# Two batches, then one, then one: another order of the MLPs beside attention, and 24 heads without split probabilities

## The chip, the core and the metric

The kernel runs on one core of one Trainium2 chip. The metric is device time in microseconds (us), from three runs of the same program. The profile and the trace come from a fourth execution. The engines are named as in the profile: PE (TensorE; PEld is its weight load), DVE (VectorE), ACT (ScalarE), POOL (GpSimd), SP (the queue that issues every DMA here).

## What is computed

Attention over 4 batches of 12 heads, 448 rows of 64, with normalised queries and keys; its output, 1792 rows of 768, goes through two MLPs.

```python
q_n, k_n = rmsnorm(q, g_q), rmsnorm(k, g_k)
scores = q_n @ k_n.T / sqrt(64)
attn = exp(scores - max)
attn = attn / (attn.sum(-1) + 1e-9)
x = attn @ v                          # 4 x 448 rows, 12 heads x 64 = 768 columns
h = x @ w_in                          # 768 -> 2048
x = maximum(0.01 * h, h) @ w_out      # 2048 -> 768
a, b = x @ w1, x @ w2                 # 768 -> 1024, twice
out = (a * b @ w3) @ w_out2           # 1024 -> 1024 -> 768
```

The MLP weights come in as float64.

## The kernel before

**Split products.** PE multiplies in a reduced float32 (`F32R`). To keep float32 accuracy, an operand is split into a high part, its rounding, and a low part, the rest; a product is then three matmuls, high by high, low by high and high by low (`group`, lines 516 to 518). ACT makes the high part, DVE or POOL the low part by a subtraction (`subtract`, line 183; `split` for activations).

**Attention**, one head at a time (`attention_steps`). Step s issues the values of head s - 2, the transposes of the probabilities of head s - 1, and the scores of head s, each in four chunks of 112 rows, then loads and preparation of later heads. `scores` (lines 263 to 276): two matmuls into `ps`, DVE scales them to `p`, ACT takes the exponent. `p_transpose` (line 307): four PE transposes into `pt`, of which there are two buffers; then either ACT copies `pt` to `pth` and DVE subtracts to get `ptl`, or, for the first `WHOLE` heads, one copy, by DVE for two chunks and by ACT for two, keeps the probabilities in full float32. `values`: split heads take eight `F32R` matmuls of 128 columns of weights, `[vh | vl]`, into `po` (line 361), and the two halves are added; the first `WHOLE` heads take four float32 matmuls on unsplit values `v_whole` (line 349). For split heads the values `v` themselves are split by ACT and POOL (`vs`). Normalised outputs of batches 0 and 1 are split at once into the tiles `xh`, `xl` of that batch; those of batches 2 and 3 go to `xd` in DRAM and are read back when their MLP begins.

**Weights.** `Weights` hands out tiles of 128 by 768 or 128 by 512, in the order in which a list names them. A wide (float64) tile is turned into float32 in two halves: per half two operations on ACT (lines 457, 462), two on POOL (458, 463), one on DVE (459); the result is written to DRAM (`kept_...`) for the next pass. Every tile is then split into `wh` on ACT (line 479) and `wl`, on POOL for wide ones, else on POOL or DVE in turn. Two tiles are made ahead; there are three buffers each of `raw`, `wh` and `wl`.

**The MLPs.** First, `combine_weights` multiplies the last two weight matrices (`pw`, 384 matmuls of 384 columns). `first_mlp` has four groups; each takes four tiles of w_in to four hidden blocks (`t`, `y`, `gh`, `gl`), then six tiles of w_out, added to `acc`. `second_mlp` has two groups of eight tiles of w1 and w2 and six of the combined weights `wc`. A tile serves as many batches as go together: `product` multiplies it into one `ps_mm` (three buffers) for each. A batch needs 1008 MLP matmuls of 448 columns.

**What sets the order.** `fill` walks through the attention steps and issues a plan's MLP work between them, evenly over the plan's slots (a slot is one head's ten steps). A scheduler then orders each engine's instructions by a timeline that it makes at build time, by readiness and the priorities in `PRIORITY`; on the chip each engine runs its list in that order. Before, `COMBINE_SLOTS` puts the combining beside heads 5 to 16, `early` two groups of batch 0's first MLP up to slot 25, `late` the same groups of batch 1 and then everything else of batches 0 and 1 beside the other heads, and `rest`, batches 2 and 3 together, behind attention.

Of the kernel before, what the change touches and what calls it, by code (L numbers as in the profile page):

```python
# [17 lines left out]
B, H, S, D = 4, 12, 448, 64  # L18
# [6 lines left out]
NG = 4  # L25
# [3 lines left out]
PB = 2  # L29
KH2 = K2 // 2  # L30
NO = DM // P
NH = B * H
# [4 lines left out]
KEYS_AHEAD = 5  # L37
GROUPS = {0: 2, 2: 2, **{i: 4 for i in range(4, 48, 4)}}
MAX_GROUP = 4
WHOLE = 8  # L40
COMBINE_SLOTS = 5, 17
EARLY = 2
PRIORITY = dict(
    values=200, p_transpose=600, scores=600, prep=600, load=100, statistics=100, keys=50
)
# [3 lines left out]
def attention_then_moe(  # L49
# [41 lines left out]
    def copy(eng, out, x):  # L91
        if eng == "A":
            nc.scalar.activation(out, x, AF.Copy)  # L93
        elif eng == "V":
            nc.vector.tensor_copy(out, x)
        else:
            nc.gpsimd.tensor_scalar(out, x, 1.0, 1.0, op0=ALU.mult, op1=ALU.mult)
# [73 lines left out]
    def load_v(i):  # L171
        if i >= NH:
            return
        b, j = divmod(i, H)
        if i < WHOLE:
            heads[i]["v"] = att.tile([CP, NCH, D], F32, tag="vs", name="v_whole")
# [65 lines left out]
    def v_split(i):  # L242
        if not 0 <= i < NH or i < WHOLE:
            return
        h = heads[i]
        h["vs"] = att.tile([CP, NCH, 2, D], F32R, tag="vs", name="vs")
        copy("A", h["vs"][:, :, 0], h["v"])
        subtract("P", h["vs"][:, :, 1], h["v"], h["vs"][:, :, 0])
# [49 lines left out]
    def p_transpose(i, kc):  # L298
        if not 0 <= i < NH:
            return  # L300
        h = heads[i]
        tags = ("pth",) if i < WHOLE else ("pth", "ptl")
        dt = F32 if i < WHOLE else F32R
        h[f"pt{kc}"] = tuple(att.tile([CP, S], dt, tag=tag, name=tag, bufs=3) for tag in tags)
# [9 lines left out]
        def natural(x):  # L314
            return x.rearrange("k (p c) -> k p c", c=NCH)

        if i < WHOLE:
            copy("VVAA"[kc], natural(h[f"pt{kc}"][0]), pt)
# [15 lines left out]
    def values(i):  # L334
# [11 lines left out]
        x = h["x"]  # L346
        if i < WHOLE:
            for kc in range(NCH):
# [174 lines left out]
    def combine_weights(ws, hi, lo):  # L523
        def last(half):
            for _ in range(KH2):
                while ws.ready <= ws.taken:
                    with tc.high_priority(CONVERT_PRIORITY if ws.ready else 0):
                        next(ws.pieces)
                    yield CONVERT_NS
                ws.take()  # L530

        n = DM // 2
        for k in range(K2):
            ps = [ps_mm.tile([P, 512], F32, tag="mm", name="pw") for _ in range(2)]
            for half in range(2):
                if k == 0:
                    yield from last(half)
                w = ws.take()
                js = range(half * KH2, (half + 1) * KH2)
                for e in range(2):  # L540
                    cols = slice(e * n, (e + 1) * n)
                    xs = [(hi[:, j, cols], lo[:, j, cols]) for j in js]
                    yield from group(ws, ps[e], n, w, xs, first=half == 0, last=half == 1)
            for e in range(2):
                o = att.tile([P, S], F32, tag="t", name="wo", bufs=1)[:, :n]
                nc.scalar.activation(o, ps[e][:, :n], AF.Copy)  # L546
                nc.sync.dma_start(
                    wc[3 * e : 3 * e + 3, :, k].rearrange("m p c -> p m c"),
                    o.rearrange("p (m c) -> p m c", m=3),
                )  # L550
# [102 lines left out]
    def sources(plan):  # L653

        kept = {}
        for f, bs, g in plan:
            if f is first_mlp:
                tiles = [w_in[g * KG + m] for m in range(KG)] + [w_out[g, m] for m in range(NO)]
            else:
                tiles = [w12[g * KH2 + m // 2, m % 2] for m in range(2 * KH2)]  # L660
            if (f, g) in kept:
                yield from ((k, False, None, None) for k in kept[f, g])
            else:
                kept[f, g] = [
                    dram.tile([P, w.shape[1] // 2], F32, name=f"kept_{f.__name__}{g}_{i}")
                    for i, w in enumerate(tiles)
                ]
                yield from ((w, True, k, None) for w, k in zip(tiles, kept[f, g]))
            if f is second_mlp:
                for m in range(NO):  # L670
                    w = wc[m, :, g * KH2 : (g + 1) * KH2].rearrange("p k c -> p (k c)")
                    yield w, False, None, None

    def plan_ns(plan):
        n = {first_mlp: KG * KD + NO * KG, second_mlp: 2 * KH2 * KD + NO * KH2}
        return sum(3 * S * NS * len(bs) * n[f] for f, bs, _ in plan)
# [22 lines left out]
    per_slot = 2 * NCH + 2  # L699
    slots = COMBINE_SLOTS  # L700

    def fill(gen, total, span, until, begin=0):

        spent, n = 0.0, 0
        done = False
        while True:
            at = next(steps, None)
            n += 1
            while not done and spent < total * (n - begin) / span:
                c = next(gen, None)  # L710
                if c is None:
                    done = True
                else:
                    spent += c
            if at is None or at == until:
                break
        for _ in gen:
            pass

    parts_of = [(first_mlp, g) for g in range(NG)] + [(second_mlp, g) for g in range(2)]  # L720
    early = [(f, (0,), g) for f, g in parts_of[:EARLY]]
    late = [(f, (1,), g) for f, g in parts_of[:EARLY]]
    late += [(f, (0, 1), g) for f, g in parts_of[EARLY:]]
    rest = [(first_mlp, (2, 3), g) for g in range(NG)]
    rest += [(second_mlp, (2, 3), g) for g in range(2)]

    def run(pool, ws, plan):
        for f, bs, g in plan:
            yield from f(pool, ws, bs, g)

    with tc.tile_pool(name="comb", bufs=1) as pool:
        hi = pool.tile([P, K2, DM], F32R, name="lasth")
        lo = pool.tile([P, K2, DM], F32R, name="lastl")
        ws = Weights(
            [
                w
                for k in range(K2)
                for h in range(2)
                for w in [
                    (w_last[j], True, None, (hi[:, j], lo[:, j]))  # L740
                    for j in range(h * KH2, (h + 1) * KH2)
                    if k == 0
                ]
                + [(w3t[k, h], True, None, None)]
            ]
            + list(sources(early + late + rest))
        )
        n = slots[1] - slots[0]
        fill(combine_weights(ws, hi, lo), comb_ns, n * per_slot, slots[1], slots[0] * per_slot)
    pool = ctx.enter_context(tc.tile_pool(name="mlp", bufs=1))  # L750
    n = PB * H + 1
    fill(run(pool, ws, early), plan_ns(early), (n - slots[1]) * per_slot, n)
    fill(run(pool, ws, late), plan_ns(late), (B - PB) * H * per_slot, None)
    fill(run(pool, ws, rest), plan_ns(rest), 1, None)


# [42 lines left out]
```

## Time and profile before

| | |
|---|---|
| median of 3 runs | 1305.79 us (1301.84 to 1306.22) |
| the profiled execution | 1304.23 us |
| its span, first to last instruction | 1302.3 us |
| mean granted clock of PE | 0.963 |
| busy: PE, DVE, ACT, POOL | 1198.4, 691.5, 705.9, 710.4 us |

Busy time of PE counts each matmul from its start to its modelled end, and matmuls overlap. So the useful measure is how far apart matmuls start. The granted clock is 1.00 for 2.4 GHz and 0.50 for 1.2 GHz; between the two it is a mean over a stretch. The rows on which the prediction rests stand in a section of their own below.

### The profile page before, as it was taken

The numbers are of one execution on the slowest core, as the hardware profiler recorded it, in microseconds if no ns is written. First come the engines' busy times: TensorE is split into PE (matmuls) and PEld (weight loads), VectorE is DVE, ScalarE is ACT, GpSimd is POOL, SyncE is SP. The second block draws the span as 40 slices with busy tenths as digits, with TensorE's granted clock in tenths as the row PEclk, the third lists the DMA queues.
The fourth block names the chain that finished last, engine by engine and source line by source line (L and its number), as shares of the span: only waits on it lengthen the run. The fifth ranks groups of instructions, "written<-read, shape, count | busy, mean of one in ns | idle before, by whom it ended". The sixth has DMA issues, their size and how long they took to land.

```text
span 1302.3 us, 18390 instructions
## 1 busy us (share of the span) xinstructions
PE 1198.4 (92%) x5960; PEld 1046.6 (80%) x5960; DVE 691.5 (53%) x1323; ACT 705.9 (54%) x1551; POOL 710.4 (55%) x723
## 2 busy tenths in 40 slices
PE   3988988997789999979988999999999999999998
PEld 2436877776679778868877998999999999999998
DVE  6786676777878697755884445333123232211112
ACT  6776677788758576656755576433331323323220
POOL 6787666898844369866986357444131314421120
PEclk8789998998889999999988999999999999999999
DMA  8677656667665456654555244144212121211112
GB/s 240 174 176 205 174 168 191 189 203 210 186 188 161 125 166 182 205 165 135 159 150 184 75 129 139 59 145 131 65 41 66 41 65 45 73 45 60 59 37 93
DMA packets 108576, 172.67 MB, mean 133 GB/s; under 512 B 23776, under 2 KB 62656, under 8 KB 108480
## 3 DMA queue, kind: packets, MB, share of 16 engines
q1 hardware_dynamic: 108480, 171.50, 45.5%
q8 instruction: 47, 0.77, 0.2%
q14 instruction: 49, 0.40, 0.1%
HBM read 130.45 MB, written 30.45 MB: 124 GB/s over the span
## 4 chain that ended last, share of the span: by engine, by line
PE 52%; DMA 16%; DVE 11%; POOL 7%; issue 6%; ACT 4%; SPq 2%; POOLq 0%; DVEq 0%; ACTq 0%
PE ps_mm L516 15%; PE ps_mm L517 15%; PE ps_mm L518 15%; DVE raw L459 3%; DMA w<-w 3%; DMA ks<-kt_sb 2%; DMA w<-w_out 2%; POOL raw L463 2%; PE pt L307 2%; DVE p L267 2%; PE po L361 2%; DMA kt_sb<-kt 2%; DMA rk<-rs 2%; POOL wl L183 1%; DMA w<-w_in 1%
## 5 line engine op out<-in xcount | busy, mean ns | idle before, releaser
L516 PE MATMUL ps_mm<-xh,wh 128*128 128x448 f32 x768 | 284.7, 371 | 0.7 <-ACT wo L546 0.7
L517 PE MATMUL ps_mm<-xl,wh 128*128 128x448 f32 x768 | 284.5, 371 | 0.0
L518 PE MATMUL ps_mm<-xh,wl 128*128 128x448 f32 x768 | 283.5, 370 | 0.0
L183 POOL TENSOR_TENSOR wl<-raw,wh 128x512 fp32r<-128x512 f32 (+1 forms) x105 | 164.7, 1568 | 180.7 <-ACT wh L479 163.0
L183 POOL TENSOR_TENSOR gl<-y,gh 128x448 fp32r<-128x448 f32 x96 | 113.3, 1181 | 192.8 <-ACT gh L93 189.4
L516 PE MATMUL ps_mm<-gh,wh 128*128 128x448 f32 x576 | 210.7, 370 | 5.3 <-ACT wh L479 2.5
L479 ACT ACTIVATE wh<-raw 128x512 fp32r<-128x512 f32 (+1 forms) x172 | 122.9, 715 | 164.9 <-PE ps_mm L517 159.4
L518 PE MATMUL ps_mm<-gh,wl 128*128 128x448 f32 x576 | 211.0, 369 | 0.0
L517 PE MATMUL ps_mm<-gl,wh 128*128 128x448 f32 x576 | 210.6, 368 | 0.0
L463 POOL TENSOR_TENSOR raw<-raw,w 128x384 uint32<-128x384 uint32 (+1 forms) x160 | 157.2, 993 | 42.6 <-DVE raw L459 35.1
L307 PE MATMUL pt<-ident,p 112*112 112x112 f32 x768 | 117.9, 279 | 44.5 <-DVE ptl L183 27.2
L516 PEld LDWEIGHTS ps_mm<-xh,wh 128*128 128x128 f32 x768 | 146.4, 191 | 12.8 <-ACT wo L546 1.1
L459 DVE SCALAR_TENSOR_TENSOR raw<-raw,w 128x384 uint32<-128x384 uint32 (+1 forms) x160 | 127.6, 813 | 54.3 <-POOL w L458 50.3
L517 PEld LDWEIGHTS ps_mm<-xl,wh 128*128 128x128 f32 x768 | 146.8, 191 | 11.8
L518 PEld LDWEIGHTS ps_mm<-xh,wl 128*128 128x128 f32 x768 | 146.3, 191 | 12.0
L307 PEld LDWEIGHTS pt<-ident,p 112*112 112x112 f32 x768 | 90.0, 142 | 81.9 <-DVE ptl L183 32.5
L276 ACT ACTIVATE p<-p,low 112x448 f32<-112x448 f32 x192 | 126.9, 662 | 48.8 <-DVE p L267 48.7
L267 DVE TENSOR_SCALAR_CACHE_REDUCE p<-ps,rs 112x448 f32<-112x448 f32 x192 | 125.3, 676 | 39.3 <-PE ps L264 22.6
L183 DVE TENSOR_TENSOR wl<-raw,wh 128x512 fp32r<-128x512 f32 (+1 forms) x67 | 58.4, 872 | 141.0 <-ACT wh L479 139.7
L462 ACT ACTIVATE w<-w 128x384 uint32<-128x384 uint32 (+1 forms) x160 | 78.5, 492 | 94.2 <-DMA w<-w 32.9
L183 DVE TENSOR_TENSOR ptl<-pt,pth 112x448 fp32r<-112x448 f32 x160 | 96.9, 617 | 58.6 <-ACT pth L93 57.6
L516 PEld LDWEIGHTS ps_mm<-gh,wh 128*128 128x128 f32 x576 | 109.3, 190 | 17.7 <-ACT wh L479 3.2
(75 smaller groups left out, 1991.0 us busy)
## 6 DMA issues: line engine op xcount, KB each, us to landing
w<-w_in SPq DMA_DIRECT2D x32, 384.0 KB, 4.7
w<-w_out SPq DMA_DIRECT2D x48, 256.0 KB, 3.7
w<-w SPq DMA_DIRECT2D x32, 384.0 KB, 4.3
qk_sb<-qk SPq DMA_DIRECT2D x48, 224.0 KB, 3.9
qt_sb<-qt SPq DMA_DIRECT2D x96, 112.0 KB, 3.2
raw<-kept_first_mlp SPq DMA_DIRECT2D x24, 384.0 KB, 3.5
raw<-kept_first_mlp SPq DMA_DIRECT2D x36, 256.0 KB, 2.7
w<-w3t SPq DMA_DIRECT2D x32, 256.0 KB, 3.7
```

The source lines that it names most:

```text
L183: e.tensor_tensor(out, x, y.bitcast(F32), op=ALU.subtract)
L267: nc.vector.tensor_scalar(p, ps, h["scale"][:, c : c + 1], None, op0=ALU.mult, op1=ALU.min, accum_out=low,)
L276: exps[i] = nc.scalar.activation(p, p, AF.Exp, bias=low, scale=-1.0, accum_out=h["sum"][:, c : c + 1])
L307: nc.tensor.transpose(pt[:, c * CP : (c + 1) * CP], h["p"][c][:, kc * CP : (kc + 1) * CP], ident[:CP, :CP],)
L361: nc.tensor.matmul(po[:, :S], v, h[f"pt{kc}"][e], start=(kc == 0 and e == 0), stop=(kc == NCH - 1 and e == 1),)
L459: nc.vector.scalar_tensor_tensor(top, top, 3, high, op0=ALU.logical_shift_left, op1=ALU.bitwise_or)
L462: nc.scalar.activation(low, low, AF.Copy, scale=2.0**-29)
L463: nc.gpsimd.tensor_tensor(top, top, low, op=ALU.add)
L479: nc.scalar.activation(flat[0], x, AF.Copy)
L516: nc.tensor.matmul(ps[:, :n], wh[:, k], xh, start=(first and k == 0), stop=False)
L517: nc.tensor.matmul(ps[:, :n], wh[:, k], xl, start=False, stop=False)
L518: nc.tensor.matmul(ps[:, :n], wl[:, k], xh, start=False, stop=end)
```

## The change

`WHOLE` goes from 8 to 24, so heads 8 to 23 (the rest of batch 0, and batch 1) keep their probabilities and values unsplit. The combining is spread over slots 5 to 24 in place of 5 to 17. The plans `early`, `late` and `rest` go; three others come, each with both MLPs whole: batches 0 and 1 together over slots 25 to 37, batch 2 alone over slots 37 to the end of attention, batch 3 alone behind it. Each plan passes through all the weights: wide tiles in the first, kept float32 tiles in the two others. Batches 2 and 3 now alternate between the two sets of activation tiles.

```diff
-WHOLE = 8
-COMBINE_SLOTS = 5, 17
-EARLY = 2
+WHOLE = 24
+COMBINE_SLOTS = 5, 24
+MLP_SLOTS = 25, 37, NH + 2
...
-    parts_of = [(first_mlp, g) for g in range(NG)] + [(second_mlp, g) for g in range(2)]
-    early = [(f, (0,), g) for f, g in parts_of[:EARLY]]
-    late = [(f, (1,), g) for f, g in parts_of[:EARLY]]
-    late += [(f, (0, 1), g) for f, g in parts_of[EARLY:]]
-    rest = [(first_mlp, (2, 3), g) for g in range(NG)]
-    rest += [(second_mlp, (2, 3), g) for g in range(2)]
+    def whole(*bs):
+        return [(first_mlp, bs, g) for g in range(NG)] + [(second_mlp, bs, g) for g in range(2)]
+
+    plans = whole(0, 1), whole(2), whole(3)
...
-            + list(sources(early + late + rest))
+            + list(sources([part for plan in plans for part in plan]))
...
-    n = PB * H + 1
-    fill(run(pool, ws, early), plan_ns(early), (n - slots[1]) * per_slot, n)
-    fill(run(pool, ws, late), plan_ns(late), (B - PB) * H * per_slot, None)
-    fill(run(pool, ws, rest), plan_ns(rest), 1, None)
+    fill(iter(()), 0, 1, MLP_SLOTS[0])
+    for plan, begin, end in zip(plans, MLP_SLOTS, MLP_SLOTS[1:] + (None,)):
+        span = (end - begin) * per_slot if end else 1
+        fill(run(pool, ws, plan), plan_ns(plan), span, end)
```

In the built order, these are PE's instructions at the scores of head 21, before. `xh` and `wh` are the high parts of activations and weights in the first MLP.

```order
L307 MATMUL pt<-ident,p 112x112 x5
L361 MATMUL po<-ptl,vs 128x448
L307 MATMUL pt<-ident,p 112x112 x4
L516 MATMUL ps_mm<-xh,wh 128x448
L517 MATMUL ps_mm<-xl,wh 128x448
L307 MATMUL pt<-ident,p 112x112 x4
L361 MATMUL po<-pth,vs 128x448
L361 MATMUL po<-ptl,vs 128x448
```

The same place of the changed kernel's PE order:

```order
L263 MATMUL ps<-ks,qh 112x448
L264 MATMUL ps<-ks,ql 112x448
L307 MATMUL pt<-ident,p 112x112 x8
L263 MATMUL ps<-ks,qh 112x448
L264 MATMUL ps<-ks,ql 112x448
L349 MATMUL po<-pth,v_whole 64x448 x2
L307 MATMUL pt<-ident,p 112x112 x3
L349 MATMUL po<-pth,v_whole 64x448
```

MLP matmuls no longer stand between the transposes, and the values are float32 matmuls. On PE, 72 MLP matmuls stand ahead of the last scores of head 26, in place of 338, and 2607 ahead of those of head 47, in place of 1694; the combining ends among the scores of head 18, in place of head 16.

On DVE near head 20, before (`raw` is a weight tile that is being turned into float32, `rs` and `rt` belong to the statistics of later heads):

```order
L459 SCALAR_TENSOR_TENSOR raw<-raw,w_3592 128x384
L183 TENSOR_TENSOR ptl<-pt,pth 112x448
L267 TENSOR_SCALAR p,low<-ps,rs 112x448
L107 TENSOR_SCALAR rs<-ss 112x32
L267 TENSOR_SCALAR p,low<-ps,rs 112x448
L459 SCALAR_TENSOR_TENSOR raw<-raw,w_3594 128x384
L110 TENSOR_SCALAR rs<-rs 112x32
L459 SCALAR_TENSOR_TENSOR raw<-raw,w_3660 128x384
L183 TENSOR_TENSOR ptl<-pt,pth 112x448
```

and of the changed kernel:

```order
L144 TENSOR_SCALAR rs<-rs 112x16
L267 TENSOR_SCALAR p,low<-ps,rs 112x448
L95 COPY pth<-pt 112x448 x2
L267 TENSOR_SCALAR p,low<-ps,rs 112x448
L230 SCALAR_TENSOR_TENSOR kt_sb<-kt_sb,gqk,rk_sb 128x448
```

The weights' halves are gone from DVE here, and a copy stands where a subtraction that waits for ACT's copy stood.

Last, PE behind attention in the changed kernel, where batch 3's hidden blocks of a group end (the numbers are buffers: `gh_12866` is the last hidden block, `wh_12821`, `wh_12848` and `wh_12879` are three weight tiles):

```order
L517 MATMUL ps_mm_12891<-gl_12809,wh_12848 128x448
L518 MATMUL ps_mm_12891<-gh_12808,wl_12849 128x448
L516 MATMUL ps_mm_12912<-gh_12692,wh_12879 128x448
L517 MATMUL ps_mm_12912<-gl_12693,wh_12879 128x448
L516 MATMUL ps_mm_12870<-gh_12866,wh_12821 128x448
L516 MATMUL ps_mm_12891<-gh_12866,wh_12848 128x448
L518 MATMUL ps_mm_12912<-gh_12692,wl_12880 128x448
L516 MATMUL ps_mm_12912<-gh_12750,wh_12879 128x448
```

Three products with three weight tiles are open at once there, with their matmuls on the last hidden block put back.

## Rows read from the trace of the kernel before

**Rows 1.** The page's first part: busy us (share of the span) xinstructions.

```profile
PE 1198.4 (92%) x5960; PEld 1046.6 (80%) x5960; DVE 691.5 (53%) x1323; ACT 705.9 (54%) x1551; POOL 710.4 (55%) x723
```

**Rows 2.** Busy us by stretch, clock, DMA: 50 us of the tail.

```profile
950.00:1000.00 50.00, 50.00 (x248) 46.35 (x247) 13.75 (x22) 14.03 (x24) 13.66 (x11) 1.00 0.18 51
```

**Rows 3.** PE in order of time: start, us, instruction, count.

```profile
149.85 0.34 PE L518 MATMUL pw<-lasth,wl 128*128 128x384 f32 x1
150.03 0.35 PE L516 MATMUL pw<-lasth,wh 128*128 128x384 f32 x1
...
151.85 0.93 PE L307 MATMUL pt<-ident,p 112*112 112x112 f32 x8
...
58.96 1.72 PE L349 MATMUL po<-pth,v_whole 112*64 112x448 f32 x4
```

**Rows 4.** By stage: PE, PEld, DVE, ACT, POOL busy, clock, DMA share, GB/s.

```profile
27.00:109.00 82.00, 70.08 (x265) 37.31 (x266) 65.78 (x138) 61.77 (x148) 68.43 (x71) 0.82 0.71 185
109.00:400.00 291.00, 249.23 (x1297) 214.10 (x1296) 217.00 (x452) 214.54 (x519) 211.09 (x238) 0.93 0.66 188
400.00:828.00 428.00, 400.00 (x2047) 354.28 (x2046) 278.67 (x523) 274.18 (x618) 283.47 (x290) 0.97 0.50 149
828.00:1302.00 474.00, 470.52 (x2330) 435.68 (x2328) 114.15 (x171) 138.19 (x236) 129.78 (x104) 1.00 0.22 68
```

**Rows 5.** By stage, instructions on tile ps_mm alone (PE, PEld, DVE, ACT).

```profile
109.00:400.00 291.00, 87.44 (x358) 69.12 (x359) 10.38 (x17) 8.83 (x17) 0.93 0.66 188
400.00:828.00 428.00, 328.30 (x1379) 260.54 (x1377) 38.56 (x63) 27.18 (x51) 0.97 0.50 149
828.00:1302.00 474.00, 468.83 (x2298) 431.31 (x2297) 69.39 (x112) 40.78 (x76) 1.00 0.22 68
```

**Rows 6.** By stage, instructions on tile pw alone (PE, PEld, ACT).

```profile
27.00:109.00 82.00, 11.00 (x55) 9.47 (x56) 0.48 (x1) 0.82 0.71 185
109.00:400.00 291.00, 67.20 (x331) 58.11 (x329) 7.31 (x15) 0.93 0.66 188
```

**Rows 7.** The same for line 307, the transposes (PE, PEld).

```profile
27.00:109.00 82.00, 19.63 (x106) 13.14 (x106) 0.82 0.71 185
```

**Rows 8.** Waits of PE: us, times, longest; 109 to 400, then 400 to 828 us.

```profile
PE pt L307 <- DVE ptl L183: 17.1, 11, 4.8
PE ps L263 <- DVE p L267: 11.2, 6, 3.3
...
PE pt L307 <- DVE ptl L183: 10.1, 9, 2.1
```

**Rows 9.** Groups by line, attention: busy us, mean ns | idle before.

```profile
L183 DVE TENSOR_TENSOR ptl<-pt,pth 112x448 fp32r<-112x448 f32 x160 | 96.9, 617 | 58.6 <-ACT pth L93 57.6 <-PE ps_mm L517 0.7
L95 DVE COPY pth<-pt 112x448 f32<-112x448 f32 x16 | 9.4, 612 | 0.0
L93 ACT ACTIVATE pth<-pt 112x448 fp32r<-112x448 f32 x160 | 83.2, 534 | 19.3 <-PE pt L307 16.7 <-PE po L361 2.3
L183 POOL TENSOR_TENSOR vs<-v_sb,vs 112x256 fp32r<-112x256 f32 x40 | 30.3, 757 | 18.1 <-ACT vs L93 15.9 <-PE pt L307 2.0 <-DMA ks<-kt_sb 0.2
```

**Rows 10.** The same view, POOL's work on weights and hidden blocks.

```profile
L458 POOL TENSOR_SCALAR w<-w 128x384 f32<-128x384 f32 x80 | 44.2, 569 | 21.1 <-ACT raw L457 20.8
L463 POOL TENSOR_TENSOR raw<-raw,w 128x384 uint32<-128x384 uint32 x80 | 91.8, 1159 | 25.4 <-DVE raw L459 20.2 <-DVE rs L116 1.8 <-DMA rk<-rs 1.6
L183 POOL TENSOR_TENSOR wl<-raw,wh 128x768 fp32r<-128x768 f32 x45 | 84.2, 1872 | 103.5 <-ACT wh L479 85.7 <-DMA kt_sb<-kt 6.7 <-DMA qt_sb<-qt 5.2
L183 POOL TENSOR_TENSOR gl<-y,gh 128x448 fp32r<-128x448 f32 x96 | 113.3, 1181 | 192.8 <-ACT gh L93 189.4 <-DMA raw<-kept_first_mlp 2.4 <-DMA w<-w_out 1.0
```

**Rows 11.** Stretches as in rows 4, within 400 to 828 us.

```profile
400.00:457.00 57.00, 54.20 (x296) 48.34 (x295) 41.88 (x89) 39.14 (x89) 22.34 (x21) 1.00 0.52 144
457.00:641.00 184.00, 166.47 (x843) 146.09 (x841) 133.74 (x242) 118.00 (x276) 140.64 (x154) 0.97 0.56 166
714.00:828.00 114.00, 113.18 (x602) 102.55 (x602) 54.92 (x113) 72.35 (x159) 63.43 (x63) 1.00 0.34 108
```

## The prediction

> **What bounds the kernel now.** I read the page's first part, then the span cut into stages, then the counts of each kind of matmul in those stages, then who PE waited for. PE is busy 92% of the span, no other engine over 55% [rows 1]. But "busy" counts matmuls that overlap or run at half clock, so I count PE's useful time instead: instructions times the spacing at which they run when nothing is in the way. In the dense tail 248 matmuls of 448 columns start in 50 us, 0.2016 us each [rows 2]. Matmuls `pw` of 384 columns start 0.18 us apart, and eight transposes take 0.93 us with the last one's tail, so about 0.1 us each [rows 3].
>
> The stages are those of [rows 4 to 7]. Up to 27 us is start-up. 27 to 109 us holds 106 transposes; a head has 16, so 6.6 heads, and 55 `pw`. 109 to 400 us holds 1297 matmuls: 358 of the MLPs, 331 `pw` and 608 others, half of them transposes (a split head has 16, with 8 scores and 8 values): 19 heads, 8 to 26. Useful there: 358 and 304 by 0.2016, 331 by 0.175, 304 by 0.096 us = 72 + 61 + 58 + 29 = 220 us of 291. **Lost: 71 us.** 400 to 828 us: 1379 MLP matmuls and 668 others: 278 + 67 + 32 = 377 of 428, lost 51. From 828 us: 2298 MLP matmuls = 463 of 474, with some 5 us for the last of attention and 2 for the end: lost about 4. So PE sets the time, and what can be won is its loss while attention runs beside it. In 109 to 400 us its largest wait is a transpose waiting for DVE's `ptl` (the slot `pt` comes free only when both halves of the split probability are made): 17.1 us, 11 times; next, scores waiting for DVE's `p`, 11.2 us [rows 8].
>
> **The change part by part.** Its sum is made against the profiled span, 1302.3 us; the profiled execution took 1.9 us more, and the median is 1.6 us above that execution.
>
> *Unsplit heads 8 to 23, on PE.* Removed for each of 16 heads: 8 `po` matmuls of 448 columns, 8 by 0.2016 = 1.6 us. Added: 4 full-precision ones, each of which the trace records twice. Four such records take 1.72 us with the last one's tail [rows 3], so a head's eight take at most 3.4 us; without the tail nearer 3.0. I take 3.2: 16 by 1.6 = **+25 us** of useful time (22 to 29). Nothing hides it, since PE is the bound.
>
> *The same heads on the other engines.* Per head four `ptl` at 0.617 and the final add leave DVE, two copies `pth` at 0.612 come to it: at least 1.2 us less. ACT loses two `pth` at 0.534 and a `vs`; POOL loses its `vs`, 0.757 [rows 9]. These engines are not the bound; the worth lies in waits. The order on DVE shows one copy of `pt` where the subtraction `ptl` stood behind ACT's copy, so the 17.1 us wait has no cause for these heads.
>
> *What leaves heads 8 to 26.* By the changed order 72 MLP matmuls stand on PE up to head 26's scores, where 338 stood before; 266 by 0.2016 = 54 us of matmuls go to later, which alone changes nothing. With them go the 20 wide weight tiles of the first two groups. A w_in tile costs POOL two halves of 0.569 + 1.159 and a low part of 1.872, 5.3 us [rows 10]; a w_out tile has two thirds of the columns, so 3.6 by estimate. 8 by 5.3 + 12 by 3.6 = 86 us leave POOL, which was busy 211 of 291 us (DVE 217, ACT 215 [rows 4]); some 110 us stay. PE has 220 - 54 + 25, about 190. So PE leads the other engines clearly, as it did in 400 to 457 us, with 54 of 57 us busy, and in 714 to 828, with 113 of 114 [rows 11]; in 109 to 400 it hardly led. I take a loss of 16% (heads 18 to 26 have almost no filler, so each PE wait there is lost): 35 of 225 us. **71 to 35: -36 us.** Bounds: 18 (a loss of 9%, more than those two stretches show in idle time) and 64 (only part of the `ptl` waits goes).
>
> *Batches 0 and 1 together beside heads 25 to 38, batch 2 beside the rest.* By the order 2535 MLP matmuls stand between the scores of head 26 and of head 47, 1356 before. Count and spacing stay, so useful time only moves forward from the tail. Loss: 51 us in 400 to 828 before, nearly all in stretches with wide tiles (457 to 641 us: PE 166 of 184 busy, POOL 141 [rows 11]). After, all 56 wide MLP tiles stand there. In the first MLP a weight group for two batches is 288 matmuls, 58 us, and costs POOL 4 by 5.3 + 6 by 3.6 + 8 `gl` by 1.181 = 52 us [rows 10], near the bound. But only 12 heads share some 460 us, about half the density of before, and the longest waits were of attention's instructions [rows 8]. I take 38 us for this and 8 for batch 2's heads, which read kept float32 weights: 51 to 46, **-5 us** (-31 to +29).
>
> *Weights three times.* By the code, tiles to be split rise from 180 to 228: 48 more kept loads, as many entries on SP's queue, and 48 splits on ACT and on DVE or POOL. They lie beside batches 2 and 3, where 828 to 1302 us shows DVE at 114, ACT at 138, POOL at 130 of 474 us and the DMA at 0.22 [rows 4]: hidden, at zero. If that cover went, a tile late by 2 us would stop PE at once. On SP's queue these loads stand among attention's own only beside heads 39 to 47.
>
> *The tail, batch 3 alone.* At each group's end a single batch waits for its chain `t`, `y`, `gh`, `gl`. The order fills this with three products of the next weights; but then three weight pairs are in use, and the fourth must be split behind them, 1 to 2 us by the split's own rows. Six such places: **+7 us** (0 to 15).
>
> Sum: 1302.3 + 25 - 36 - 5 + 7 = 1293 us of span; with 3.5 us to the median, **1296**, 0.7% faster.
>
> **The rivals.** (1) *The early heads get no faster; slower than before.* In 27 to 109 us, heads already unsplit took 82 us for 6.6 heads; less 55 `pw` by 0.175, 10.9 us each. At that pace heads 8 to 26 take 19 by 10.9 + 58 (`pw`) + 15 (72 MLP matmuls) = 280 us where I have 225: 1351; with half of that excess, 1324. For it: it is the same code. Against it: that stage also splits the wide last weights and starts up. It decides from 8.8 us a head, net of filler (1312 us).
>
> (2) *The clock.* In 27 to 109 us the granted clock is 0.82 on average, a mix of 1.2 and 2.4 GHz, behind PE's waits; from 828 us, without waits, 1.00 [rows 4]. Heads 18 to 26, left without filler, hold about 9 by 6.4 + 15 = 73 us of useful work; at 0.82 that is 89: 1312 us. Against it: 109 to 400 us had 0.93 with more waits per matmul than I expect. The Trainium skill (TensorE: Matmul & The Clock Gate, section HAM oscillation — how this bites in real kernels) says that waits between bursts of matmuls drop the clock to half, so that each burst begins slow; by that rule this rival comes, and the trace agrees in the early stage.
>
> (3) *POOL becomes the bound beside batches 0 and 1.* First MLP: 4 by 52 + 14 for `xl` + 7 heads by 3.5 = 246 us of POOL. At the 76% that it reached in 457 to 641 us [rows 11] this takes 324 us, where PE needs 232 + 33 = 265: a loss of 59 where my 38 has 30 for it: 1325. For it: 52 against 58 us a group. Against: weights are split ahead while heads run.
>
> (4) *Better:* heads 8 to 26 lose 18 and batches 0 and 1 lose 20: 1296 - 17 - 18 = 1261.
>
> (5) *The change doesn't do what it says:* MLP work is scheduled back among heads 18 to 26. The order rules it out but for 72 matmuls.
>
> **How the numbers follow.** About 0.5% (6.5 us) is what a measurement of this kernel can tell from no change. Forecast, with its parts off by some us: 0.47, of which 0.30 under 1299 and 0.17 from 1299 to 1312. Case (4): 0.18. Slower by (1): 0.15; by (3): 0.12. Case (2): 0.06, half of it over 1312. Case (5): 0.02, within 0.5%. So faster 0.48, same 0.22, slower 0.30. The range takes in case (4) and the slow cases up to half of (1)'s excess and some: 1261 to 1334; the forecast's own is 1278 to 1314.
>
> **What would show it.** Head 26's probabilities should end near 335 us (about 400 before), without `ptl` waits ahead of head 24; over 370 us means rival 1, at a lower clock rival 2. From there to head 47 PE should be at clock 1.00 nearly throughout; waits of `ps_mm` for `wh`, `wl` or `gl` mean rival 3. The dense tail from head 47 on should be about 300 us, with 248 matmuls in 50 us; fewer means that a single batch's weights come late. The prediction is wrong if the 25 us of full-precision matmuls aren't there, or if waits on DVE's `p` replace those on `ptl`.

## The result, and the profile after

The changed kernel takes 1323.06 us (median of 4 runs, 1321.87 to 1325.6) against 1304.69 beside it: 1.015 times, 95% interval 1.012 to 1.017. It is slower by 18 us; 1296 was forecast. Its profiled span is 1320.4 us against 1302.3.

Its page, first part, as [rows 1]:

```profile
PE 1229.1 (93%) x5960; PEld 1028.0 (78%) x5960; DVE 686.3 (52%) x1307; ACT 722.7 (55%) x1551; POOL 721.7 (55%) x723
```

Its stages, as [rows 4]: heads 8 to 26; heads 27 to 38, beside batches 0 and 1; heads 39 to 47, beside batch 2; the tail. (Heads 0 to 7 end at 111 us in place of 109.)

```profile
109.00:357.00 248.00, 225.42 (x1057) 151.97 (x1056) 151.60 (x359) 156.20 (x381) 127.64 (x148) 0.97 0.59 157
357.00:836.00 479.00, 450.62 (x2235) 403.62 (x2234) 250.76 (x425) 265.38 (x578) 337.89 (x349) 0.98 0.50 150
836.00:1019.00 183.00, 180.59 (x953) 164.84 (x952) 109.84 (x214) 108.68 (x226) 71.86 (x60) 0.99 0.42 121
1019.00:1320.00 301.00, 294.06 (x1431) 265.09 (x1429) 94.62 (x132) 114.39 (x193) 100.41 (x75) 1.00 0.37 113
```

The same stretches for `ps_mm` alone, as [rows 5] (PE, PEld, DVE, ACT); then the first stretch for `pw`, for line 307 (transposes) and for line 349 (full-precision values):

```profile
109.00:357.00 248.00, 27.68 (x116) 21.05 (x117) 2.42 (x4) 2.66 (x5) 0.97 0.59 157
357.00:836.00 479.00, 413.84 (x1853) 350.35 (x1852) 53.02 (x87) 35.28 (x67) 0.98 0.50 150
836.00:1019.00 183.00, 154.74 (x670) 125.20 (x669) 24.70 (x40) 12.17 (x23) 0.99 0.42 121
1019.00:1320.00 301.00, 291.37 (x1399) 260.44 (x1397) 37.30 (x61) 25.82 (x49) 1.00 0.37 113
...
109.00:357.00 248.00, 70.84 (x332) 58.06 (x330) 7.21 (x15) 0.97 0.59 157
...
109.00:357.00 248.00, 45.37 (x304) 33.76 (x304) 0.97 0.59 157
...
109.00:357.00 248.00, 65.93 (x140) 15.52 (x140) 0.97 0.59 157
```

With the prediction's spacings, PE's useful time among heads 8 to 26 is 116 by 0.2016 + 332 by 0.175 + 304 by 0.096 + 140 by 0.4 + 165 others by 0.2016 = 200 of 248 us: **48 lost, where 35 were forecast.** Counted the same way, 68 were lost before; the prediction's 71 took the full-precision values of heads 6 and 7, 12 records in this stretch, as split ones. Beside heads 27 to 47 it is 430 of 479 and 177 of 183: **56 lost with the fractions, 51 before, 46 forecast.** In the tail about 286 of 301 with the end in it: 15 lost, 7 before. So PE has 25 us more to do, as worked out, and loses only 7 us less in all: 18 us net, the difference of the two spans.

Heads 8 to 26 are two different stretches: heads 8 to 17, beside the combining, and heads 18 to 26, before and then after, as [rows 4]:

```profile
109.40:264.60 155.20, 136.07 (x724) 116.93 (x723) 108.84 (x236) 109.96 (x272) 106.80 (x126) 0.96 0.66 184
264.60:399.80 135.20, 112.57 (x572) 96.58 (x571) 107.96 (x217) 103.98 (x247) 103.78 (x112) 0.90 0.67 192
...
111.00:262.50 151.50, 134.75 (x631) 93.20 (x631) 83.77 (x202) 90.61 (x222) 83.65 (x101) 0.95 0.63 173
262.50:357.20 94.70, 88.87 (x417) 56.95 (x416) 68.01 (x158) 63.81 (x155) 42.18 (x48) 1.00 0.51 130
```

Heads 18 to 26 lost 35 us before and lose 15 now: PE is idle there for 6 us in place of 23, and at full clock throughout. Heads 8 to 17 lose 34 us, and lost 33 before: the change shows no gain there.

Who PE waited for, heads 8 to 26, then 27 to 38 (us, times, longest):

```profile
PE po L349 <- ACT x L93: 9.7, 7, 3.1
PE pt L307 <- ACT pth L93: 3.3, 2, 2.2
PE ps L263 <- DVE p L267: 2.7, 4, 1.5
...
PE pt L307 <- DVE ptl L183: 1.6, 1, 1.6
...
PE pt L307 <- DVE ptl L183: 6.7, 5, 3.0
PE ps L263 <- DVE p L267: 5.8, 4, 2.7
PE ps_mm L516 <- DVE acc L587: 5.6, 4, 2.6
PE ps_mm L516 <- DVE y L606: 4.9, 3, 2.4
```

The `ptl` wait of 17.1 us [rows 8] is gone among the early heads, as forecast, but for 1.6 us at 338 us; a new one stands there, values that wait for ACT to empty the one buffer `po`. Before, the `ptl` wait stood mostly beside heads 18 to 26; here it is for heads 8 to 17, then for heads 18 to 26:

```profile
PE pt L307 <- DVE ptl L183: 3.0, 4, 1.5
...
PE pt L307 <- DVE ptl L183: 14.1, 7, 4.8
```

The new wait of 9.7 us stands beside heads 8 to 17 alone.

### The profile page after: what moved, and what is told of

Same layout as the page of the kernel before. It is cut to its first block, busy times and chain, and to the rows that moved or that the text cites. A ratio compares the mean times of both kernels' runs of the same rounds, so it can differ in the third digit from the quotient of the medians.

```text
span 1320.4 us, 18548 instructions
## 1 busy us (share of the span) xinstructions
PE 1229.1 (93%) x5960; PEld 1028.0 (78%) x5960; DVE 686.3 (52%) x1307; ACT 722.7 (55%) x1551; POOL 721.7 (55%) x723
## 4 chain that ended last, share of the span: by engine, by line
PE 47%; DMA 21%; POOL 9%; issue 8%; DVE 7%; ACT 5%; SPq 3%; POOLq 0%; ACTq 0%; DVEq 0%
PE ps_mm L516 13%; PE ps_mm L518 13%; PE ps_mm L517 13%; DMA w<-w_out 3%; POOL raw L463 3%; DMA w<-w 2%; PE pt L307 2%; POOL wl L183 2%; DMA w<-w3t 2%; DMA ks<-kt_sb 2%; DMA w<-w_in 2%; DVE raw L459 2%; DMA x<-xd 2%; DMA rk<-rs 2%; PE po L361 2%
## 5 line engine op out<-in xcount | busy, mean ns | idle before, releaser
L183 POOL TENSOR_TENSOR wl<-raw,wh 128x512 fp32r<-128x512 f32 (+1 forms) x121 | 191.3, 1581 | 219.6 <-ACT wh L479 183.0
L479 ACT ACTIVATE wh<-raw 128x512 fp32r<-128x512 f32 (+1 forms) x220 | 157.0, 719 | 179.0 <-PE ps_mm L517 130.1
L516 PE MATMUL ps_mm<-gh,wh 128*128 128x448 f32 x576 | 211.4, 378 | 16.9 <-DVE y L606 7.3
L459 DVE SCALAR_TENSOR_TENSOR raw<-raw,w 128x384 uint32<-128x384 uint32 (+1 forms) x160 | 133.7, 855 | 108.8 <-POOL w L458 105.4
L463 POOL TENSOR_TENSOR raw<-raw,w 128x384 uint32<-128x384 uint32 (+1 forms) x160 | 153.9, 973 | 35.8 <-DVE raw L459 33.2
L183 DVE TENSOR_TENSOR wl<-raw,wh 128x512 fp32r<-128x512 f32 (+1 forms) x99 | 91.3, 924 | 123.9 <-ACT wh L479 123.1
L307 PE MATMUL pt<-ident,p 112*112 112x112 f32 x768 | 115.0, 270 | 22.0 <-DVE ptl L183 8.3
L307 PEld LDWEIGHTS pt<-ident,p 112*112 112x112 f32 x768 | 86.8, 137 | 61.3 <-DVE ptl L183 11.1
L518 PEld LDWEIGHTS ps_mm<-gh,wl 128*128 128x128 f32 x576 | 109.8, 191 | 11.3 <-DVE wl L183 2.1
```

The costliest lines, as they stand in the source:

```text
L183: e.tensor_tensor(out, x, y.bitcast(F32), op=ALU.subtract)
L307: nc.tensor.transpose(pt[:, c * CP : (c + 1) * CP], h["p"][c][:, kc * CP : (kc + 1) * CP], ident[:CP, :CP],)
L459: nc.vector.scalar_tensor_tensor(top, top, 3, high, op0=ALU.logical_shift_left, op1=ALU.bitwise_or)
L463: nc.gpsimd.tensor_tensor(top, top, low, op=ALU.add)
L479: nc.scalar.activation(flat[0], x, AF.Copy)
L516: nc.tensor.matmul(ps[:, :n], wh[:, k], xh, start=(first and k == 0), stop=False)
```

## Experiments

The losses below are worked out like those above, from each run's own trace; stages end with the last probabilities of heads 7, 17, 26 and 47. "Time" is the median, "before" the kernel before beside it.

| run | time | before | useful | lost: heads 8-17 | 18-26 | both | 27-47 | tail |
|---|---|---|---|---|---|---|---|---|
| before | 1304.7 | | 1123 | 33 | 35 | 68 | 51 | 7 |
| changed | 1323.1 | 1304.7 | 1148 | 34 | 15 | 48 | 56 | 15 |
| e1 unsplit alone | 1324.8 | 1301.6 | 1148 | 27 | 29 | 56 | 59 | 7 |
| e2 plans alone | 1321.4 | 1301.6 | 1123 | 40 | 35 | 75 | 55 | 13 |
| e4 two and two | 1329.8 | 1301.6 | 1148 | 27 | 16 | 43 | 66 | 16 |
| e10 changed, no conversion | 1276.6 | 1299.6 | 1148 | 29 | 16 | 45 | 13 | 14 |
| e11 before, no conversion | 1247.6 | 1299.6 | 1123 | 24 | 22 | 46 | 12 | 7 |

In e4 heads 8 to 17 have the changed kernel's code and slots, and lose 27 us where it loses 34. So differences of some 7 us in one stretch show little by themselves.

**The parts alone.** Theory S: the unsplit heads cost; theory M: the plans do.

```diff
# e1, on the kernel before          # e2, on the changed kernel
-WHOLE = 8                          -WHOLE = 24
+WHOLE = 24                         +WHOLE = 8
```

> The kernel before with WHOLE = 24 alone: its own plans for the combining and the MLPs stay. Theory S (the full-precision matmuls cost PE their 25 us, and the shorter waits of heads 8 to 23 give back less than that; the plans cost little): 1304.7 + 25 less some 10 to 20 of waits, so 1310 to 1320. Theory M (the new MLP plans are what costs; unsplit heads by themselves pay for their 25 us, since the ptl waits of 17 us and 7 us of half clock go): 1295 to 1305.

> The changed kernel with WHOLE = 8: its plans alone. PE has 25 us less to do than in the changed kernel. Theory S: 1300 to 1310, no more than 5 us from before. Theory M: 1320 or more, since single batches beside batch 2's and batch 3's weights and wide tiles beside batches 0 and 1 stay; the changed trace has 56 us of PE loss there and 13 in the tail, against 51 and 6 before, so M has to find the rest in heads 8 to 26, which would again lose 70 us.

e1: 1324.76 us, ratio 1.017 (1.013 to 1.021). e2: 1321.43 us, 1.015 (1.011 to 1.019). Each part costs about 20 us, and both together no more. So neither theory holds alone (e1 lies above both of its ranges, e2 in theory M's), and the parts are not additive. By the table, unsplit heads in the old plans give back 12 us beside heads 8 to 26 for their 25, and lose 7 later. The new plans with split heads lose 7 us more beside heads 8 to 26, 4 beside the others and 6 in the tail. Only in the new plans do the unsplit heads return 27 us, about what they cost, and some 20 of these stand beside heads 18 to 26: those lose 29 us in e1, 35 in e2 and 15 only with both parts.

The granted clock has a share in this. Here are heads 8 to 26 in e1, then in e2:

```profile
110.10:400.80 290.70, 265.66 (x1232) 184.93 (x1231) 180.78 (x396) 188.11 (x455) 193.14 (x217) 0.96 0.62 177
...
108.40:348.50 240.10, 202.11 (x1009) 167.80 (x1009) 177.10 (x402) 168.78 (x414) 135.68 (x155) 0.88 0.58 160
```

A mean of 0.88 means that e2 runs for 57 of these 240 us at 1.2 GHz, against 41 of 290 before and 14 of 246 in the changed kernel. PE is idle for 38 us in e2, 42 before and 23 in the changed kernel. So split heads without filler do what rival 2 feared, and unsplit ones do not.

**Is the full-precision work on the path?** One pass on rounded probabilities and values, as its expectation says:

```diff
-        dt = F32 if i < WHOLE else F32R
+        dt = F32R
...
+        if i < WHOLE:                  # v is rounded once, low part left out
+            x = att.tile([CP, NCH, D], F32R, tag="vs", name="v_whole")
+            copy("A", x, h["v"])
```

> The changed kernel, but for its 24 unsplit heads the probabilities and values are rounded and multiplied in one pass, with no low parts: this part of the computation is left out, and ACT makes one rounding copy of v more. PE has 24 by 4 by 0.6 = 58 us less to do. Theory S2 (the full-precision matmuls lie on the path, all of them): 1320 - 58 = 1262, a little over by ACT's copies. Rival C (heads 8 to 26 are bound by the chain through DVE and ACT, and full-precision matmuls only fill time in which PE would wait): 1285 to 1310.

1284.86 us, at the edge of rival C's range, 38 less than the changed kernel by the medians and 34 by each one's ratio to the kernel before, for 58 us less of PE work (96 matmuls here, 192 records of twice that spacing there). So some three fifths to two thirds lie on the path; the rest PE would wait anyway, now for DVE's `p`, 16.9 us in 12 waits among heads 8 to 26.

**The new wait on `po`.** Its copy given to DVE; then a second buffer for odd heads:

```diff
# e3
-            copy("A", x[mine(i)], po[:D, :S])
+            copy("V", x[mine(i)], po[:D, :S])
# e9
+        if i < WHOLE and i % 2:
+            po = ps_mm.tile([P, 512], F32, tag="mm", name="po")
...
```

> The changed kernel, but for unsplit heads the copy of po to x is made by DVE and not by ACT. In the changed trace PE's longest wait among heads 8 to 26 is a values matmul for ACT's copy, 9.7 us in 7 waits, since po has one buffer. If that wait is what took the place of the ptl wait, DVE's copy (DVE has the shorter queue there, 152 of 248 us busy against ACT's 156, so hardly) gives back up to 10 us: 1313 to 1318. If DVE is as late as ACT: 1323, with the wait named DVE x.

> The changed kernel, with the values of odd unsplit heads written to one of the three buffers that the combining and the MLPs use, so that two heads' values can be open at once. Theory W (the loss of 33.9 us that stayed beside heads 8 to 17 is the values' wait for ACT's copy out of the one buffer po, 9.7 us in 7 waits, and what follows from it): loss there falls to 22 to 26 us, 1308 to 1314 in all. Rival C (the chain p, exponent, transposes, copies sets the pace, and the wait goes to the next link): 1318 to 1325, with PE waiting for DVE's p or for a copy pth in place.

e3: 1319.04 us, at most 4 gained, within the intervals (1.012, 1.008 to 1.017, against 1.015). e9: 1323.57 us, none: the wait is gone, and PE waits for a copy `pth` (10.3 us) and DVE's `p` (8.7 us) in its place. That the chain sets the pace, and the wait was its last link only, fits this, but no run shortens the chain itself. Nor are the two runs clean. Heads 8 to 17 lose 28 and 29 us in them, 5 or 6 less than in the changed kernel, but e4 and e10, which leave `po` alone, lose 27 and 29. And the edits reach heads 0 to 7, which lose 60 and 62 us in place of 54. The edit for heads 8 to 23 alone was not tried.

**Weights three times, batches alone.**

```diff
-MLP_SLOTS = 25, 37, NH + 2
+MLP_SLOTS = 25, NH + 2
...
-    plans = whole(0, 1), whole(2), whole(3)
+    plans = whole(0, 1), whole(2, 3)
```

> The changed kernel with two plans in place of three: batches 0 and 1 together over slots 25 to the end of attention, batches 2 and 3 together behind it; unsplit heads stay. Weights are read twice. If single batches cost (48 more weight tiles to split, group ends with one batch's chain), this gains the 8 us of the tail and a little more: 1308 to 1316. If they don't, the same time, 1320 to 1326; it could lose, since 23 heads share batch 0 and 1's wide tiles and no MLP work of batch 2 stands beside attention.

1329.77 us, above both ranges. Its tail has no wait at all, where the changed kernel's from 1040 us on has 42 spacings over 0.215 us, 7.7 us in all, at group ends. But its matmuls there stand 0.2065 us apart on average (243 in 50 us, below, against 248 in [rows 2]), at the same clock and without waits: some 9 us over 2275 matmuls, for which I have no cause. Beside heads 27 to 47 it loses 10 us more than the changed kernel.

```profile
950.00:1000.00 50.00, 50.00 (x243) 45.41 (x243) 9.39 (x14) 17.82 (x31) 14.16 (x11) 1.00 0.17 48
```

**What makes the loss beside heads 27 to 38: wide tiles.** Conversion of the 56 wide MLP tiles left out but for one step of five, so that the MLPs run on weights that are not converted:

```diff
+            if t < 24:
...
+            else:
+                nc.scalar.activation(out, signed, AF.Copy, scale=2.0**-112)
```

> The changed kernel without the turning of the MLPs' wide weights into float32, but for one of its two ACT operations on each half: the other ACT operation, both on POOL and the one on DVE are left out, for 56 tiles, so the MLPs are computed on wrong weights. Theory T (wide tiles make the loss beside batches 0 and 1, wherever they stand): the loss beside heads 27 to 38 falls from 49.5 to about 15 us, some 3% like that of stretches without wide tiles: 1285 to 1292. Rival G (the loss there is from hidden blocks, acc and attention's chains, with or without wide tiles): 1310 to 1320.

> The kernel before without the same operations, for the same 56 tiles (MLPs on wrong weights). Theory T, wide tiles cost the same in either plan: as much less as the changed kernel loses, 1270 to 1280, from heads 18 to 41. If the new plan makes them dearer (they meet batches 0 and 1 in one place): less gain here than there, 1285 to 1295. Rival G: 1295 to 1302.

1276.62 and 1247.63 us. The stretch of heads 27 to 38, first of e10, then of e11:

```profile
352.00:792.00 440.00, 437.85 (x2250) 401.31 (x2249) 159.24 (x326) 230.11 (x482) 191.97 (x154) 1.00 0.53 161
...
376.00:591.00 215.00, 211.90 (x1133) 191.40 (x1133) 137.98 (x290) 147.22 (x331) 106.34 (x92) 1.00 0.65 191
```

PE is busy 438 of 440 and 212 of 215 us, at clock 1.00 throughout; 7 us are lost in each of these stretches, 49 and 33 with conversion. By the spans of single executions, conversion costs 1320.4 - 1274.9 = 46 us in the changed kernel and 1302.3 - 1241.0 = 61 before; but e11's profiled execution was its fastest and 5 us under its median. By the medians, as ratios to the kernel before beside each, it is 43 and 52. So wide tiles make the loss beside heads 27 to 38, as theory T says for e10. Both times are below every range that was expected, and for e11 theory T's equal price falls too: the new plan makes wide tiles cheaper, by some 9 us (16 by the spans), where each ratio's interval is 3 to 4 us to either side.

With conversion out, heads 8 to 26, first in e10, then in e11, lose 45 and 46 us:

```profile
111.00:352.00 241.00, 220.29 (x1038) 146.90 (x1037) 142.14 (x346) 148.63 (x360) 106.42 (x117) 0.98 0.60 164
...
110.00:376.00 266.00, 241.98 (x1284) 209.30 (x1283) 180.98 (x408) 195.00 (x470) 149.48 (x154) 0.96 0.71 203
```

So in the old plans, split heads lose no more than unsplit ones in the new, once wide tiles are out. But the absence of wide tiles is not by itself what the changed kernel gained: e2 has as few of them there (line 459 runs 34 times beside heads 8 to 26, 36 times in the changed kernel and 63 before), and its split heads, without filler, lose 75.

**What in the conversion costs.** Single steps moved or left out. The step of e5, e6, e17 and e18 is line 458, on POOL.

```diff
# e5 (changed), e6 (before): the step to DVE; e17 (before), e18 (changed): to ACT
-            nc.gpsimd.tensor_scalar(signed, signed, 0.0, 1.0, op0=ALU.mult, op1=ALU.mult)
+            nc.vector.tensor_scalar(signed, signed, 0.0, 1.0, op0=ALU.mult, op1=ALU.mult)
+            nc.scalar.activation(signed, signed, AF.Copy, scale=0.0)
# e13 (before): lines 462 and 463 only for the first 24 tiles
+            if t < 24:
# e14 (before), e15 (changed): the low part of wide MLP tiles
-            subtract("P" if wide or t % 3 == 0 else "V", flat[1], x, flat[0])
+            subtract("P" if t < 24 or t % 3 == 0 else "V", flat[1], x, flat[0])
```

> The changed kernel with one of the two POOL operations on each half of a wide weight tile (line 458, 0.57 or 0.46 us on POOL) given to DVE, which does the next operation on that half itself. Theory H (beside batches 0 and 1, DVE stands in its queue waiting for POOL in front of line 459, 109 us in all against 54 before, and y and acc, for which PE waits there, are queued behind): without that wait the loss beside heads 27 to 38 falls from 49.5 to 35 us or less, 1305 to 1312. Rival P (PE waits there because of the amount of work on DVE and POOL or of attention's own chains, not because of the order in the queue): 1318 or more, since DVE gets 160 operations of 0.3 to 0.5 us more.

> The kernel before with the same operation given to DVE. Theory H: its wide tiles have the same wait, 54 us in all, so it gains about half as much, 1295 to 1300. Rival P: 1304 to 1312.

> The kernel before, with the last two steps of turning a wide MLP tile into float32 left out for 56 tiles (ACT's and POOL's, lines 462 and 463, which add the last three bits of each weight): the weights are truncated to 21 bits. POOL has 112 operations of 0.83 or 1.16 us less, some 110 us. Theory V (the 61 us that conversion costs before come from the amount of POOL's work, whose lateness makes DVE and ACT wait in their queues): most of it returns, 1255 to 1270. Rival L (each hop between engines costs, five per half): two of five hops go, 1275 to 1285.

> The kernel before, with the low part of the 56 wide MLP tiles made by DVE in place of POOL, as for two of three kept tiles (for every third it stays on POOL). POOL has some 37 operations of 1.34 or 1.87 us less, 60 us; DVE as many of 0.8 to 1.0 more. All bits are kept. Theory V: 1280 to 1293, a faster kernel. Rival L: no hop goes, and DVE's queue, with attention's p and ptl in it, is longer: 1300 to 1312.

> The same edit in the changed kernel, where conversion costs 46 us by the run without it. Theory V: 1300 to 1312; DVE has more room there (251 of 479 us busy beside heads 27 to 38), POOL least (338). Rival L: 1318 to 1328.

> The kernel before with line 458 (the first of POOL's two operations on each half of a wide tile) made by ACT, which makes the operation ahead of it. In the traces DVE's line 459, with two inputs in SBUF, takes 0.55 us when POOL rests and 1.0 on average, up to 3.8, when POOL works beside it, while DVE's operations with an input in PSUM take 0.62 either way. Theory K (the loss comes from POOL's hops and from DVE being held up by POOL): one hop of five goes, POOL has 82 us less to do, so a fifth to a third of 61 us is gained: 1280 to 1291, all bits kept. Rival Q (it comes from the length of the queues: ACT gets 160 operations of 0.5 us, with p, pth and gh behind them): 1300 to 1315.

> The same edit in the changed kernel. Theory K: a fifth to a third of 46 us: 1306 to 1313. Rival Q: 1320 to 1330.

e17 and e18 differ in one more thing: their wide weights come out wrong. That ACT's form loses the sign is the likely reason; no run shows it apart.

| run | moved | time | ratio to before |
|---|---|---|---|
| e5, changed | POOL's step to DVE | 1328.4 | 1.022 (1.019 to 1.025) |
| e6, before | the same | 1311.3 | 1.010 (1.007 to 1.013) |
| e14, before | POOL's low parts to DVE | 1303.8 | 1.003 (1.001 to 1.006) |
| e15, changed | the same | 1325.0 | 1.020 (1.015 to 1.025) |
| e17, before | POOL's step to ACT | 1325.4 | 1.018 (1.016 to 1.021) |
| e18, changed | the same | 1333.2 | 1.025 (1.023 to 1.027) |
| e13, before | two steps left out | 1280.7 | 0.986 (0.982 to 0.989) |

POOL was rid of 51 to 79 us of busy time in e6, e14 and e17, and none got faster. The pages of e6, e14 and e17, beside [rows 1]:

```profile
PE 1202.2 (92%) x5960; PEld 1047.1 (80%) x5960; DVE 728.0 (56%) x1483; ACT 709.6 (54%) x1551; POOL 639.2 (49%) x563
...
PE 1198.0 (92%) x5960; PEld 1042.7 (80%) x5960; DVE 706.2 (54%) x1360; ACT 709.3 (54%) x1551; POOL 658.9 (51%) x686
...
PE 1206.1 (91%) x5960; PEld 1049.6 (79%) x5960; DVE 687.5 (52%) x1323; ACT 766.2 (58%) x1711; POOL 631.0 (48%) x563
```

So theories H, V and K fall: moving POOL's work to another engine brings nothing. That POOL's work has no price of its own is not shown, since no run takes it away without giving it to another engine or, as e10, e11 and e13 do, leaving out steps of ACT too. 60 us more on ACT cost 25 us, 37 more on DVE 12, though both were busy half of the time. Removing work from ACT and POOL (e13) returned 20 us, two fifths of the 52, which is rival L's count of hops (two of five), but L does not explain e17, which takes a hop away and loses. Rival Q fits e17, e18 and e6 in its direction, though e17 and e18 lie above its ranges: conversion stands in the queues of ACT and DVE among attention's links, and lengthens them. Q was not tested with POOL's and ACT's share apart, so how the 52 us divide stays open.

**Attempts at a faster kernel.** On the kernel before:

```diff
# e8                 # e12, with e9's second buffer    # e16
-WHOLE = 8           -WHOLE = 8                        -CONVERT_PRIORITY = 100
+WHOLE = 2           +WHOLE = 12                       +CONVERT_PRIORITY = 20
```

> The kernel before with WHOLE = 2 in place of 8: six heads fewer unsplit. If an unsplit head costs what the 16 of the run of the kernel before with WHOLE = 24 cost (23 us more, 1.4 us each), 6 by 1.4 = 8 us are gained: 1296. If in the first stage, where PE waits anyway and the clock is low, PE's longer values are free and the splits are not, it is slower: 1306 to 1320.

> An attempt at a faster kernel: the one before with WHOLE = 12 and the values of odd unsplit heads in a second buffer as above. WHOLE = 2 cost 32 us and WHOLE = 24 cost 23, so the best lies between. If four heads more still gain their ptl waits (17.1 us stood among heads 8 to 26) against 4 by 1.6 us of PE: 1290 to 1297. If WHOLE = 8 is past the best point already: 1302 to 1310.

> An attempt at a faster kernel: the one before with CONVERT_PRIORITY 20 in place of 100, so that the scheduler puts conversion behind statistics and keys in each engine's queue. If what costs is attention's instructions waiting behind a conversion that itself waits for POOL: 1285 to 1297. If tiles come late in return: 1305 to 1320.

1331.23, 1320.69 and 1311.99 us, against 1298.88, 1299.56 and 1300.28: all slower, e8 and e12 above both of their ranges. Six heads more split at the start cost 32 us, although PE has 10 us less to do; 20 of them are lost beside heads 0 to 7. Here are 50 us of them, before and in e8, at a lower clock and with PE idle for 17 us in place of 7:

```profile
50.00:100.00 50.00, 42.90 (x170) 22.25 (x168) 39.66 (x82) 38.10 (x92) 43.73 (x46) 0.90 0.74 187
...
50.00:100.00 50.00, 32.85 (x131) 24.62 (x132) 35.72 (x76) 35.53 (x81) 36.61 (x37) 0.71 0.63 170
```

No version that computes everything in full beat the kernel before. e13 did, with three bits of the weights less, and e7, the changed kernel with the low parts of 24 heads' probabilities and values left out.

## Why the prediction was wrong

1. **Full-precision values, +25 us: right, at the upper end of its bounds.** Line 349 took, for PE, as many records as worked out. The useful time, 1123 to 1148, counts each at the 0.40 us that was taken; where no wait stands between them and the clock is full, 131 of them stand 0.43 us apart on average in the changed kernel's trace, so 16 by 1.8 = 29 us is nearer. e7 shows that three fifths to two thirds of such work lie on the path.
2. **71 to 35 us beside heads 8 to 26, -36: the step that failed.** It was 68 to 48, -20. The mechanism that I named, no cause left for the `ptl` wait, came true. But 14.1 of the 17.1 us stood beside heads 18 to 26, and there the loss fell from 35 to 15 us. Beside heads 8 to 17 only 3.0 us stood; they lost 33 us before and lose 34 now, with a new wait of 9.7 us for `po`. I took one loss of 16% for all 19 heads, because "PE leads the other engines clearly"; it is 15% beside heads 18 to 26, which I thought the risk, and 22% beside heads 8 to 17. What keeps heads 8 to 17 slow is shown only in part: PE is idle for 17 of their 34 us, by waits that go to the next link of the chain when one is taken away (e9: `pth` and `p`), and at half clock for 14 us; the rest is matmuls that follow each other more slowly than the spacings I took. The busy share of DVE and ACT (152 and 156 of 248) was no measure of the loss. Net of filler the heads took (248 - 58 - 23) / 19 = 8.8 us each, the very point from which rival 1 was to decide; head 26 ended at 357 us, between its two signs, 335 and 370.
3. **51 to 46 us beside heads 27 to 47, -5: failed too.** It was 56, +4. My 8 for batch 2's heads was 6; my 38 for wide tiles was 49, of which e10 shows 42 to be conversion. I had cut the price for the lower density of heads; the price per tile fell only from 52/56 = 0.9 to 43/56 = 0.8 us. Rival 3 had the place, but 11 of its 29 us, and not the cause: no wait of `ps_mm` there was for `wh` or `gl` of POOL, and relieving POOL gave nothing (e15). That its time, 1325, and that of half of rival 1, 1324, are close to the measured one is luck.
4. **Weights three times at zero: right** as far as the traces show: no wait for a late load stands among PE's, and one of 1.0 us in the tail for the low part of a kept tile. **Tail +7: right in size,** 8, of which 7.7 us are gaps at group ends. Its reason shows in part: of the three gaps over 1 us, one (1.0 us of wait) is for a weight's split, and two (2.3 us) are for ACT's copy `acc`.
5. **Rival 2, the clock,** did not come: heads 18 to 26 ran at 1.00, without any stretch at half clock, where it was 0.90 before. It came in e2, the same plans with split heads, 0.88 over heads 8 to 26. The Trainium skill (TensorE: Matmul & The Clock Gate, section HAM oscillation — how this bites in real kernels) says that waits between bursts of matmuls drop the clock to half. The traces agree: beside heads 8 to 26 PE was idle for 38 us and at half clock for 57 in e2, for 23 and 14 in the changed kernel. Rival 5 was excluded by the order, and the order held: 72 MLP matmuls ran ahead of the last scores of head 26, and 116 before 357 us.

So in spans +25.4 - 20.1 + 4.3 + 8.3, and 0.2 beside heads 0 to 7, make the 18.1 us that were measured, where I had +25 - 36 - 5 + 7. The range, up to 1334, held the time; the forecast within it was a gain, since each slow case was weighed alone, and steps 2 and 3 missed toward the slow side together, by 16 and 9 us.

## What to carry to other kernels

Before you price a wait that a change takes away, see in which part of the stretch it stands: here 14 of 17 us were beside nine of the nineteen heads, and only these got faster. Beside the others PE's next wait took its place. The pace of a stretch that already runs in the new form, here 27 to 109 us, warns of that, though its 10.9 us a head were 2 too many. What costs beside a chain (here the conversion of float64 weights) costs nearly as much in another place. Two halves of a change that each lose 20 us can lose 20 together: try each half alone.

## What the runs showed of the hardware

In these traces DVE's operations with two inputs in SBUF took longer while POOL worked, and those that read PSUM did not. Here are DVE and POOL at 561 us of the changed kernel, and the matmul of PE that waited (start, us, instruction, and in brackets PE's idle time before it):

```profile
561.41 0.84 POOL L458 TENSOR_SCALAR w<-w 128x384 f32<-128x384 f32 x1
561.78 0.94 DVE L230 SCALAR_TENSOR_TENSOR kt_sb<-kt_sb,gqk,rk_sb 128x448 f32<-128x448 f32 x1
562.21 1.11 POOL L183 TENSOR_TENSOR vs<-v_sb,vs 112x256 fp32r<-112x256 f32 x1
562.65 3.84 DVE L459 SCALAR_TENSOR_TENSOR raw<-raw,w 128x384 uint32<-128x384 uint32 x1
563.28 1.83 POOL L183 TENSOR_TENSOR wl<-raw,wh 128x768 fp32r<-128x768 f32 x1
565.07 1.00 POOL L463 TENSOR_TENSOR raw<-raw,w 128x384 uint32<-128x384 uint32 x1
...
566.41 1.14 DVE L587 TENSOR_TENSOR acc<-ps_mm,acc 128x448 f32<-128x448 f32 x2
...
567.08 0.47 PE L516 MATMUL ps_mm<-xh,wh 128*128 128x448 f32 x1 [2.59 <-DVE acc L587]
```

Line 459 took 3.84 us, across three POOL instructions one behind the other; `acc` stood behind it, and PE waited 2.59 us for `acc`. Over the changed kernel the 80 such operations of 384 took 0.55 us where POOL rested (7 of them), 1.12 where POOL worked for at least half of the time (68); `acc` took 0.62 in either case (36 and 54). The Trainium skill (SBUF — State Buffer, section Who interferes with whom) says that a DVE instruction with two SBUF inputs contends with a POOL instruction that reads SBUF; the trace agrees, 0.55 against 1.12 us. Why relieving POOL brought no time all the same is not shown. In e6 and e14 what POOL gave up became DVE's, and took longer there too when POOL worked for at least half of the time: line 458 of 384 on DVE, with one input in SBUF, 0.36 us with POOL at rest and 0.78 beside it (37 and 38 in e6), `wl` of 768 0.96 and 1.47 (26 and 12 in e14). In e17 it became ACT's.
